# Weights by casting GpSimd DMAs beside Q, K and V, in place of plain loads in SP's queue cast by GpSimd

## The chip, the cores and the metric

The kernel runs on one core of one Trainium2 chip. The metric is the device time of one execution in microseconds (us); the median of three runs of the kernel before is 322.58 us (322.06 to 323.25). Engines are written as the profile writes them: PE (TensorE), with its weight loads PEld, DVE (VectorE), ACT (ScalarE), POOL (GpSimd) and SP (SyncE), which only issues DMAs here.

## The reference

Linear attention per head, a root-mean-square norm of each head's row, and then a two-layer network with an ELU between:

```python
kv  = einsum('bhsd,bhse->bhde', k, v)             # q, k, v: (8, 8, 576, 64) float32
out = einsum('bhsd,bhde->bhse', q, kv)
rms = sqrt(mean(out * out, axis=-1, keepdims=True) + 1e-06)
x   = (out / rms * g_norm)                        # heads side by side: (4608, 512)
h   = x @ w_in                                    # w_in: (512, 2048)
g   = where(h > 0, h, exp(minimum(h, 0)) - 1)
y   = g @ w_out                                   # w_out: (2048, 512), y: (4608, 512) float32
```

## The kernel before

**Tiling.** The 4608 tokens are worked on in nine groups of 512 tokens (G). Group b below 8 is the first 512 of the 576 positions of batch b; group 8 collects the last 64 positions of all eight batches. For each group the kernel computes attention (K'V of the batch, Q transposed by PE, Q times K'V, the norm, the result transposed to xT), then a first product with w_in (`mm1`, eight steps i of 256 of the 2048 columns, 16 matmuls each in bf16), the ELU, and a second product with w_out (`mm2`, 16 matmuls of 128x512 for each of four blocks of 128 tokens; `mm2_half(T, i)` does eight of them). The reduction index f of the second product, 0 to 15, runs over rows of w_out in blocks of 128; f below 4 lies in the first quarter of w_out, 12 to 15 in the last.

**Order.** A manual schedule is on: every engine runs its instructions in the order in which the program states them, and semaphores hold it only for data and for buffers. The attention of group T+1 is spread over the steps of the first product of group T by the dictionaries `steps`, and the second product of group T-1 over the same steps. For T = 0 the attention of group 1 stands in the first product of group 0 (q at step 2, kv at 3, se0 at 4, se1 at 6), and the second product of group 0 begins after step 7; after its first two halves PE transposes group 1's result (L284). Group 0's own attention (L396 to L492) is written out by hand, with `idle` matmuls on PE between its parts; its norm works on one joint tile `ss_all` for all four blocks.

**Loads.** All DMAs go out from SP, in float32, into a rotating set of six staging buffers `st` (L46, L72). The queue's order is: q, then halves of k and v of group 0 (L383 to L389), g_norm, w_in quarters 0 and 1 (`fetch_w_in`, L114), q, k and v of group 1 (`fetch`, L108), w_in 2 and 3, the four quarters of w_out (`fetch_w_out`, L122), group 2, group 3, and from then on a group for each group worked on, behind the stores of results. An issue waits until the staging buffer that it takes has been read.

**Casts.** Group 0 is cast to bf16 by DVE and ACT, part by part, as it lands. Everything else is cast by POOL through `copy_on` (L134), in the order w_in 0 and 1, group 1, w_in 2 and 3, w_out 0 to 3, group 2, and so on: four casts of 128x512 for q or a weight quarter (`cast_w_in`, L157; `cast_w_out`, L162), five for k or v.

**The ELU of a step** (L318 to L333): ACT takes exp of the step's PSUM tile (for odd steps of group 0 also relu), DVE takes min and subtract on `elu_e` (L325) and then a max or add into gT (L328), which is what the second product reads. The two PSUM tiles of `mm1` are given back by the last of these. One PSUM tile `at` (L170, two banks, a single buffer) serves all parts of the attention of groups 1 to 8 in turn.

Of the kernel before, what the change touches and what calls it, by code (L numbers as in the profile page):

```python
# [16 lines left out]
def kernel(  # L17
# [13 lines left out]
    nc = tc.nc  # L31
    P = 128
# [8 lines left out]
    KC = DM // P  # L41
# [1 line left out]
    NT = B + 1  # L43

    const = ctx.enter_context(tc.tile_pool(name="const", bufs=1))
    stage = ctx.enter_context(tc.tile_pool(name="stage", bufs=6))  # L46
    qkvp = ctx.enter_context(tc.tile_pool(name="qkvp", bufs=2))
    attp = ctx.enter_context(tc.tile_pool(name="attp", bufs=2))
    mlpg = ctx.enter_context(tc.tile_pool(name="mlpg", bufs=2))
# [18 lines left out]
    w_in_sb = const.tile([P, KC, DF], BF16, name="w_in_sb")  # L68
    w_out_sb = const.tile([P, FC, DM], BF16, name="w_out_sb")


    def stage_tile():  # L72
        return stage.tile([P, 2304], FP32, name="st", tag="st")

    raw, bf = {}, {}

    def fetch_q(b):

        st = stage_tile()[:, 0:2048]
        raw["q", b] = st  # L80
        if b < B:
            for s in range(2):
                nc.sync.dma_start(
                    out=st.rearrange("p (s h x) -> p s h x", s=2, h=4)[:, s],
                    in_=q[b].rearrange("(h s) r d -> s h r d", s=2)[s, :, 0:G, :].rearrange(
                        "h (p j) d -> p h (j d)", j=J
                    ),
                )
        else:
            sv = st.rearrange("p (i s h d) -> p i s h d", i=J, s=2, h=4)  # L90
            for t in range(B):
                for s in range(2):
                    nc.sync.dma_start(
                        out=sv[(t % 2) * 64 : (t % 2) * 64 + 64, t // 2, s],
                        in_=q[t].rearrange("(h s) r d -> s h r d", s=2)[
                            s, :, G:S, :
                        ].rearrange("h p d -> p h d"),
                    )

    def fetch_kv(name, src, b):  # L100

        st = stage_tile()
        raw[name, b] = st
        return st.rearrange("p (h x) -> p h x", h=4), src[b].rearrange(
            "h r d -> (h r d)"
        ).rearrange("(h p x) -> p h x", h=4, p=P)

    def fetch(b):  # L108
        fetch_q(b)
        for name, src in (("k", k), ("v", v)):  # L110
            out_, in_ = fetch_kv(name, src, b)
            nc.sync.dma_start(out=out_, in_=in_)

    def fetch_w_in(s):  # L114
        st = stage_tile()[:, 0:2048]
        nc.sync.dma_start(
            out=st.rearrange("p (c f) -> p c f", c=KC),
            in_=moe_w_in.rearrange("(c p) f -> p c f", p=P)[:, :, s * 512 : s * 512 + 512],
        )
        raw["wi", s] = st  # L120

    def fetch_w_out(s):  # L122
        st = stage_tile()[:, 0:2048]
        nc.sync.dma_start(
            out=st.rearrange("p (c f) -> p c f", c=KC),
            in_=moe_w_out.rearrange("(c p) f -> p c f", p=P)[:, 4 * s : 4 * s + 4, :],
        )
        raw["wo", s] = st

    def copy_on(eng, out_, in_):  # L130
        if eng is nc.scalar:
            nc.scalar.copy(out_, in_)
        else:
            eng.tensor_copy(out=out_, in_=in_)  # L134

    def q_tile(b):
        bf["q", b] = qkvp.tile([P, J, H, D], BF16, name="q_bf", tag="q")
        st = raw.pop(("q", b))
        if b < B:
            return st.rearrange("p (h j d) -> p j h d", h=H, j=J)  # L140
        return st.rearrange("p (j h d) -> p j h d", h=H, j=J)

    def kv_tile(name, b):
        bf[name, b] = qkvp.tile([P, RK, 4, D], BF16, name=f"{name}_bf", tag=name)
        return raw.pop((name, b)).rearrange("p (h j d) -> p j h d", h=4, j=RK)

    def cast_q(b, eng):
        sv = q_tile(b)
        for j in range(J):
            copy_on(eng, bf["q", b][:, j], sv[:, j])  # L150

    def cast_kv(name, b, eng):
        sv = kv_tile(name, b)
        for lo, hi in ((0, 2), (2, 4), (4, 6), (6, 8), (8, 9)):
            copy_on(eng, bf[name, b][:, lo:hi], sv[:, lo:hi])

    def cast_w_in(s, eng):  # L157
        st = raw.pop(("wi", s)).rearrange("p (c f) -> p c f", c=KC)
        for c in range(KC):
            copy_on(eng, w_in_sb[:, c, s * 512 : s * 512 + 512], st[:, c, :])  # L160

    def cast_w_out(s, eng):  # L162
        st = raw.pop(("wo", s)).rearrange("p (c f) -> p c f", c=KC)
        for c in range(KC):
            copy_on(eng, w_out_sb[:, 4 * s + c, :], st[:, c, :])


    xT = {}
# [5 lines left out]
    def kv_mm(T, kv_ps, u):  # L174

        for j in range(RK):
            for s in range(2):
                rows = slice(s * 64, s * 64 + 64)
                nc.tensor.matmul(  # L179
                    kv_ps[s][:, u * P : u * P + P],  # L180
                    lhsT=bf["k", T][rows, j, 2 * u : 2 * u + 2, :],
                    rhs=bf["v", T][rows, j, 2 * u : 2 * u + 2, :],
                    start=(j == 0),
                    stop=(j == RK - 1),
                )
# [192 lines left out]
    V, A, Q = nc.vector, nc.scalar, nc.gpsimd  # L378
# [6 lines left out]
    for u in range(2):  # L385
        for out_, in_ in halves:
            nc.sync.dma_start(
                out=out_[:, 2 * u : 2 * u + 2, :], in_=in_[:, 2 * u : 2 * u + 2, :]
            )  # L389
    g_src = bass.AP(tensor=g_norm.tensor, offset=g_norm.offset, ap=[[1, 64], [1, 1]])  # L390
    for i in range(2):
        nc.sync.dma_start(out=g_col[i * 64 : i * 64 + 64, :], in_=g_src)
    for s in range(2):
        fetch_w_in(s)

    q_st = q_tile(0)  # L396
    qt_ps = ps_m1.tile([P, 2, G], FP32, name="qt_ps", tag="mm1").rearrange(
# [4 lines left out]
    def idle(n):  # L402
        for _ in range(n):
            nc.tensor.matmul(idle_ps[:, 0, :], lhsT=ident, rhs=zeros, start=True, stop=True)  # L404
# [10 lines left out]
    kv_ps = [ps_m2.tile([P, DM], FP32, name="kv_ps", tag="mm2") for _ in range(2)]  # L415
    for u in range(2):
        for n, name in enumerate("kv"):
            for eng, js in ((V, slice(0, 5)), (A, slice(5, 9))):
                copy_on(
                    eng,  # L420
                    bf[name, 0][:, js, 2 * u : 2 * u + 2, :],
                    kv_st[n][:, js, 2 * u : 2 * u + 2, :],
                )
            if (u, n) == (0, 0):
                nc.vector.tensor_copy(out=qT0[:, 0:2, :], in_=qt_ps[:, 0:2, :])
                nc.scalar.copy(qT0[:, 2:4, :], qt_ps[:, 2:4, :])
        kv_mm(0, kv_ps, u)
        if u == 0:
            idle(6)
        for eng, l in ((V, 0), (A, 1)):  # L430
            ls = slice(l * 64, l * 64 + 64)
            for s in range(2):
                copy_on(
                    eng,
                    bd_kv[ls, 0, 2 * s + u, ls],
                    kv_ps[s][ls, u * P + l * 64 : u * P + l * 64 + 64],
                )
# [57 lines left out]
    def cast_all(b):  # L495
        cast_q(b, Q)
        if b < B:
            cast_kv("k", b, Q)
            cast_kv("v", b, Q)

    for s in range(2):
        cast_w_in(s, Q)
    fetch(1)
    cast_all(1)
    for s in range(2, 4):
        fetch_w_in(s)
    for s in range(2, 4):
        cast_w_in(s, Q)
    for s in range(4):
        fetch_w_out(s)  # L510
        cast_w_out(s, Q)
    fetch(2)
    at = attention(1)
    steps = {2: "q", 3: "kv", 4: "se0", 6: "se1"}
    for i in range(8):
        cols = (slice(0, 256), slice(256, 512)) if i == 0 else (slice(0, 512),)
# [69 lines left out]
```

## Time and profile before

| | |
|---|---|
| median of 3 runs | 322.58 us (322.06 to 323.25) |
| the profiled execution: its time, its span | 322.58 us, 320.4 us |
| busy: PE, DVE, ACT, POOL | 295.8, 179.2, 151.8, 78.4 us |
| DMA moved, and mean rate | 46.44 MB, 145 GB/s |
| first matmul of the first product | 22.03 us |
| first matmul of the second product | 45.48 us |
| DMA engines busy without a break | from 1 to about 62 us |
| granted TensorE clock | 1.000 |

The span runs from the first to the last instruction of the profiled execution; its own time is 2.18 us more. In the profile a line such as "L134 POOL CAST k_bf<-st" is a group of instructions: the line of the program (here that of the helper `copy_on`), the engine, the operation, what it writes and reads. A bracket such as "[2.28 <-POOL w_in_sb L134]" is the idle time of the engine just before it, and what is taken to have ended it; where an instruction waits for several things, the one that came last by the profile is named, which need not be the one that mattered. In the page's slices, each digit is the busy share of one fortieth of the span, about 8 us, in tenths.

### The profile page before, as it was taken

How to read it: one execution, taken by the hardware profiler on the slowest of the kernel's cores; microseconds unless marked ns; L12 is line 12 of the kernel's file. 1: busy time of each engine (PE TensorE's matmuls, PEld its weight loads, DVE VectorE, ACT ScalarE, POOL GpSimd, SP SyncE). 2: the span in 40 equal slices, each digit the busy share in tenths (PEclk: the TensorE clock that was granted, in tenths of full speed). 3: DMA queues.
4: the chain of work that ended last, by engine and by line, in shares of the span. 5: the costliest groups of instructions: out<-in, count | busy, mean ns of one | idle time of the engine just before them, and what ended most of it. 6: DMA issues, size and time to landing. Idle time of an engine off the chain costs nothing.

```text
span 320.4 us, 4746 instructions
## 1 busy us (share of the span) xinstructions
PE 295.8 (92%) x1905; PEld 149.7 (47%) x1941; DVE 179.2 (56%) x215; ACT 151.8 (47%) x215; POOL 78.4 (24%) x140
## 2 busy tenths in 40 slices
PE   8777686988899999999999999999999999999993
PEld 3443343554454445455545455545454545444441
DVE  3466584558447754775377537744874576454400
ACT  3654654356445544544544455444544545443220
POOL 0069998920026002600260045002000000000000
PEclk9999999999999999999999999999999999999999
DMA  7999999800193019302920392024201010101122
GB/s 255 354 376 389 386 374 376 314 0 2 61 354 119 25 68 349 139 4 89 368 102 2 108 363 88 0 90 99 78 1 65 2 65 2 65 0 65 68 65 65
DMA packets 28565, 46.44 MB, mean 145 GB/s; under 512 B 5504, under 2 KB 13696, under 8 KB 28544
## 3 DMA queue, kind: packets, MB, share of 16 engines
q1 hardware_dynamic: 28544, 46.14, 41.1%
q8 instruction: 15, 0.25, 0.3%
q14 instruction: 6, 0.05, 0.0%
HBM read 36.70 MB, written 9.44 MB: 144 GB/s over the span
## 4 chain that ended last, share of the span: by engine, by line
PE 78%; DMA 7%; DVE 5%; ACT 5%; issue 2%; SPq 1%; POOL 0%; DVEq 0%
PE o_ps L344 36%; PE h_ps L310 33%; DMA st<-in_moe_w_in_dram 5%; DMA st<-in_v_dram 3%; ACT elu_e L318 2%; PE at L179 2%; PE at L284 2%; DVE gT L328 2%; PE at L189 2%; PE at L201 2%; DVE ss L225 1%; DVE elu_e L325 1%; ACT sq L220 1%; DVE xs L235 1%; ACT elu_h L322 1%
## 5 line engine op out<-in xcount | busy, mean ns | idle before, releaser
L310 PE MATMUL h_ps<-xT,w_in_sb 128*128 128x512 bf16 (+1 forms) x564 | 133.8, 376 | 6.3 <-DVE gT L328 3.6
L344 PE MATMUL o_ps<-w_out_sb,gT 128*128 128x512 bf16 x562 | 133.9, 379 | 3.6 <-DVE gT L328 2.8
L318 ACT ACTIVATE elu_e<-h_ps 128x1024 bf16<-128x1024 f32 x72 | 73.5, 1020 | 50.2 <-PE h_ps L310 49.0
L344 PEld LDWEIGHTS <-gT 128*128 128x128 bf16 x576 | 56.2, 98 | 70.6 <-DVE gT L328 3.3
L328 DVE TENSOR_TENSOR gT<-elu_e,h_ps 128x1024 bf16<-128x1024 bf16 x68 | 83.0, 1221 | 7.1
L310 PEld LDWEIGHTS <-w_in_sb 128*128 128x128 bf16 x584 | 55.2, 98 | 65.2 <-issue 3.2
L325 DVE TENSOR_SCALAR elu_e<-elu_e 128x1024 bf16<-128x1024 bf16 x72 | 33.3, 462 | 87.8 <-ACT elu_e L318 87.8
L134 POOL CAST q_bf<-st 128x512 bf16<-128x512 f32 x32 | 18.9, 629 | 125.1 <-DMA st<-in_q_dram 103.4
L354 ACT COPY o_sb<-o_ps 128x512 f32<-128x512 f32 x36 | 21.0, 583 | 24.5 <-PE o_ps L344 24.5
L235 DVE TENSOR_TENSOR xs<-at,ss 128x1024 bf16<-128x1024 f32 x16 | 19.6, 1225 | 9.9 <-ACT ss L232 9.9
L220 ACT ACTIVATE sq<-at 128x1024 bf16<-128x1024 f32 (+1 forms) x18 | 17.5, 977 | 14.5 <-PE at L201 12.0
L225 DVE TENSOR_REDUCE ss<-sq 128x16 f32<-128x1024 bf16 x16 | 19.5, 1218 | 4.8 <-ACT sq L220 4.7
L134 POOL CAST k_bf<-st 128x512 bf16<-128x512 f32 (+1 forms) x35 | 20.1, 617 | 5.3 <-DMA st<-in_k_dram 4.5
L134 POOL CAST v_bf<-st 128x512 bf16<-128x512 f32 (+1 forms) x35 | 18.9, 584 | 0.7
L294 ACT ACTIVATE xT<-at,g_col 128x1024 bf16<-128x1024 bf16 x8 | 8.9, 1114 | 18.5 <-DVE xT L291 18.5
L231 ACT ACTIVATE ss<-ss,eps_col 128x16 f32<-128x16 f32 x16 | 4.9, 307 | 24.7 <-DVE ss L225 24.7
L404 PE MATMUL idle_ps<-zeros,ident 128*128 128x512 bf16 x43 | 13.3, 446 | 1.6 <-POOL ident masks.py:199 1.4
L264 ACT COPY qT<-at 128x1024 bf16<-128x1024 bf16 x8 | 8.1, 1012 | 12.3 <-DVE qT L263 12.3
L134 POOL CAST w_in_sb<-st 128x512 bf16<-128x512 f32 x16 | 9.8, 655 | 15.8 <-DMA st<-in_moe_w_in_dram 15.8
L179 PEld LDWEIGHTS <-k_bf 64*128 64x128 bf16 x288 | 8.2, 94 | 8.7 <-issue 4.1
L179 PE MATMUL at<-v_bf,k_bf 64*128 64x128 bf16 x252 | 8.3, 216 | 3.0 <-POOL w_in_sb L134 2.3
L201 PEld LDWEIGHTS <-qT 128*128 128x128 bf16 x128 | 8.4, 98 | 5.2 <-issue 1.9
(48 smaller groups left out, 117.6 us busy)
## 6 DMA issues: line engine op xcount, KB each, us to landing
st<-in_q_dram SPq DMA_DIRECT2D x16, 512.0 KB, 6.3
out_dram<-o_sb SPq DMA_DIRECT2D x16, 512.0 KB, 3.1
st<-in_k_dram SPq DMA_DIRECT2D x7, 1152.0 KB, 9.4
st<-in_v_dram SPq DMA_DIRECT2D x7, 1152.0 KB, 11.0
st<-in_moe_w_in_dram SPq DMA_DIRECT2D x4, 1024.0 KB, 12.8
st<-in_moe_w_out_dram SPq DMA_DIRECT2D x4, 1024.0 KB, 13.8
st<-in_k_dram SPq DMA_DIRECT2D x2, 576.0 KB, 7.2
st<-in_v_dram SPq DMA_DIRECT2D x2, 576.0 KB, 8.1
```

The costliest lines, as they stand in the source:

```text
L134: eng.tensor_copy(out=out_, in_=in_)
L179: nc.tensor.matmul(kv_ps[s][:, u * P : u * P + P], lhsT=bf["k", T][rows, j, 2 * u : 2 * u + 2, :], rhs=bf["v", T][rows, j, 2 * u : 2 * u + ...
L201: nc.tensor.matmul(ov[:, u, :, s, :], lhsT=qT[:, p, j * P : j * P + P], rhs=bd_kv[:, T, p, :], start=True, stop=True,)
L220: nc.scalar.activation(sq, se_ps, AF.Square)
L225: nc.vector.reduce_sum(out=ss, in_=sq.rearrange("p c (h e) -> p (c h) e", h=H), axis=AX.X)
L235: nc.vector.tensor_tensor(out=xs.rearrange("p c (h e) -> p (c h) e", h=H), in0=se_ps.rearrange("p c (h e) -> p (c h) e", h=H), in1=ss.to_b ...
L310: nc.tensor.matmul(h_ps[:, a, cs], lhsT=w_in_sb[:, c, f * P : f * P + P], rhs=x[:, c, cs], start=(c == 0), stop=(c == KC - 1),)
L318: nc.scalar.activation(e, h_ps, AF.Exp)
L325: nc.vector.tensor_scalar(out=e, in0=e, scalar1=1.0, scalar2=1.0, op0=ALU.min, op1=ALU.subtract)
L328: nc.vector.tensor_tensor(out=gT[T][:, 2 * i : 2 * i + 2, :], in0=e, in1=h, op=ALU.add if relu else ALU.max,)
L344: nc.tensor.matmul(o_ps[T, j], lhsT=gT[T][:, f, j * P : j * P + P], rhs=w_out_sb[:, f, :], start=(f == 0), stop=(f == FC - 1),)
L354: nc.scalar.copy(o_sb[T][:, j % 2, :], o_ps.pop((T, j)))
```

## The change

The weights no longer pass through staging and POOL's casts. Each quarter of w_in and w_out is loaded by one DMA issued from GpSimd's queue, which reads float32 and writes bf16 straight into `w_in_sb` or `w_out_sb`. The staging set shrinks from six buffers to three. In SP's queue, group 1 now follows group 0 directly. POOL's order becomes: a piece of group 0's V cast; w_in 0 and 1; q of group 1 cast; w_in 2 and 3; k and v of group 1 cast; w_out 0 to 3; then group 2's casts as before. The cast of the first half of group 0's V is split over three engines in place of two. The steps of group 1's attention and the norm chain are the same in both kernels.

```diff
-    stage = ctx.enter_context(tc.tile_pool(name="stage", bufs=6))
+    stage = ctx.enter_context(tc.tile_pool(name="stage", bufs=3))
...
-    def fetch_w_in(s):
-        st = stage_tile()[:, 0:2048]
-        nc.sync.dma_start(
-            out=st.rearrange("p (c f) -> p c f", c=KC),
-            in_=moe_w_in.rearrange("(c p) f -> p c f", p=P)[:, :, s * 512 : s * 512 + 512],
+    def load_w_in(s):
+        cols = slice(s * 512, s * 512 + 512)
+        nc.gpsimd.dma_start(
+            out=w_in_sb[:, :, cols], in_=moe_w_in.rearrange("(c p) f -> p c f", p=P)[:, :, cols]
         )
-        raw["wi", s] = st
...
+    def load_w_out(s):
+        fs = slice(4 * s, 4 * s + 4)
+        nc.gpsimd.dma_start(
+            out=w_out_sb[:, fs, :], in_=moe_w_out.rearrange("(c p) f -> p c f", p=P)[:, fs, :]
         )
...
-    for s in range(2):
-        fetch_w_in(s)
...
-            for eng, js in ((V, slice(0, 5)), (A, slice(5, 9))):
+            parts = ((V, slice(0, 5)), (A, slice(5, 9)))
+            if (u, n) == (0, 1):
+                parts = ((V, slice(0, 4)), (A, slice(4, 7)), (Q, slice(7, 9)))
+            for eng, js in parts:
...
+    fetch(1)
     for s in range(2):
-        cast_w_in(s, Q)
-    fetch(1)
-    cast_all(1)
+        load_w_in(s)
+    cast_q(1, Q)
     for s in range(2, 4):
-        fetch_w_in(s)
-    for s in range(2, 4):
-        cast_w_in(s, Q)
+        load_w_in(s)
+    cast_kv("k", 1, Q)
+    cast_kv("v", 1, Q)
     for s in range(4):
-        fetch_w_out(s)
-        cast_w_out(s, Q)
+        load_w_out(s)
     fetch(2)
```

More of the change, by code (lines that the diff above doesn't have):

```diff
@@ L112, in fetch @@
             nc.sync.dma_start(out=out_, in_=in_)
-    def fetch_w_in(s):
-        st = stage_tile()[:, 0:2048]
-        nc.sync.dma_start(
-            out=st.rearrange("p (c f) -> p c f", c=KC),
-            in_=moe_w_in.rearrange("(c p) f -> p c f", p=P)[:, :, s * 512 : s * 512 + 512],
-        )
-        raw["wi", s] = st
[L122 to L126, printed above, removed]
+    def load_w_in(s):
+        cols = slice(s * 512, s * 512 + 512)
+        nc.gpsimd.dma_start(
+            out=w_in_sb[:, :, cols], in_=moe_w_in.rearrange("(c p) f -> p c f", p=P)[:, :, cols]
+        )
+    def load_w_out(s):
+        fs = slice(4 * s, 4 * s + 4)
+        nc.gpsimd.dma_start(
+            out=w_out_sb[:, fs, :], in_=moe_w_out.rearrange("(c p) f -> p c f", p=P)[:, fs, :]
         )
-        raw["wo", s] = st
     def copy_on(eng, out_, in_):
@@ L155, in cast_kv @@
             copy_on(eng, bf[name, b][:, lo:hi], sv[:, lo:hi])
[L157 to L165, printed above, removed]
     xT = {}
```

## The prediction

> **What bounds the kernel now.** I read four views in this order. First the page's slices and the table of windows, to see in which stage TensorE is not full:
>
> ```profile
> 20.00:36.00 16.00, 11.41 (x107) 6.88 (x108) 8.09 (x12) 8.94 (x13) 13.58 (x24) 1.00 1.06 387
> 36.00:52.00 16.00, 10.90 (x62) 5.09 (x60) 11.49 (x13) 8.64 (x13) 14.29 (x23) 1.00 1.06 381
> 86.00:118.00 32.00, 31.74 (x211) 16.36 (x215) 19.12 (x22) 15.84 (x22) 7.78 (x14) 1.00 0.40 140
> ```
>
> Columns are the stretch, its length, busy time of PE, PE's weight loads, DVE, ACT and POOL, then clock, DMA share and GB/s. From 86 us on PE is busy 31.7 of 32 us with DMA at 40%: the change, which touches only loads and their casts, can win or lose nothing there. From 20 to 52 us PE has 9.7 us of idle, the DMA engines are saturated (share above 1, 381 to 387 GB/s) and POOL casts without a break. The change acts here, and before.
>
> Second, the chain that ended last, for what starts this stage:
>
> ```profile
> 3.34 9.12 DMA st<-in_v_dram
> 12.49 0.57 DVE v_bf L134
> ...
> 20.01 14.44 DMA st<-in_moe_w_in_dram
> 34.50 0.62 POOL w_in_sb L134
> 35.20 1.69 PE h_ps L310 x7
> ```
>
> The second half of group 0's V lands at 12.46 us, and from it a gapless chain runs to the first product at 22.03. The second piece looks as if w_in held everything until 34.5. The wait itself says less, so third, PE in that stretch:
>
> ```profile
> 33.86 1.18 PE L179 MATMUL at<-v_bf,k_bf 64*128 64x128 bf16 x36 [2.28 <-POOL w_in_sb L134]
> 35.20 1.67 PE L310 MATMUL h_ps<-xT,w_in_sb 128*128 128x512 bf16 x7 [0.16 <-POOL w_in_sb L134]
> 40.22 1.89 PE L310 MATMUL h_ps<-xT,w_in_sb 128*128 128x512 bf16 x8 [1.17 <-DVE gT L328]
> 45.48 3.19 PE L344 MATMUL o_ps<-w_out_sb,gT 128*128 128x512 bf16 x14
> 51.51 0.60 PE L344 MATMUL o_ps<-w_out_sb,gT 128*128 128x512 bf16 x2 [2.84 <-DVE gT L328]
> ```
>
> The product at 33.86 reads no w_in. It needs the one `at` buffer back from ScalarE's qT copy (32.70 + 1.01 = 33.71) and v_bf (cast by 32.12): the 2.28 us are ScalarE's, behind DVE. Only 0.16 us is a wait for w_in. The other gaps end with DVE's gT. So **the first product is paced by ScalarE and VectorE, not by weights**; weights merely arrive in time. How much in time, POOL says:
>
> ```profile
> 42.59 5.37 POOL L134 CAST w_out_sb<-st 128x512 bf16<-128x512 f32 x8 [0.42 <-DMA st<-in_moe_w_out_dram]
> ```
>
> w_out is complete at 47.96. PE starts the second product at 45.48; at 0.216 us each (8 take 1.73), its matmul f=12, first to need the last quarter, is due at 48.1. **Slack of the last weight: 0.1 us** until f=12, and 3.5 us until 51.5, when gT of the last step comes.
>
> **The Trainium skill.** "DMA: Bandwidth & Descriptors", section "SWDGE vs HWDGE vs iDMA": a casting DMA must come from GpSimd, whose descriptors are software-made, in a queue of its own; section "Issuing engines are not separate DMA queues": it shares the same 16 DMA engines. This trace has one data queue, so sharing is not shown; that the 16 are full until 62 us is. Section "Queues, rings and completion order": each engine takes turns between queues packet by packet. Packets here are rows: 8,192 of 1 KB for q, 8,192 of 2.25 KB for k and v, 4,096 of 2 KB for the weights fit the page's counts. "SBUF — State Buffer", section "Who interferes with whom": a VectorE operation in a two-port mode and a GpSimd operation exclude each other. The trace agrees: elu_e's 128x1024 TENSOR_SCALAR takes 0.42 us with POOL idle (65 to 84 us) but 0.66, 0.58, 0.69, 0.72, 0.88, 0.42, 0.59, 0.42 in the first product.
>
> **The change, part by part.**
>
> Removed: 32 weight casts on POOL of about 0.61 us, 19.6 us, all beside other work. They hold PE for 0.16 us and lengthen elu_e by 1.6 us in sum (the eight above less 8 x 0.42), of which steps 0, 2, 4 and 6 lie on the chain: 0.24 + 0.27 + 0.46 + 0.17 = 1.1 us. But POOL still casts group 1 and, earlier than before, group 2 in this stage, so about half stays: **gain 0.5 us** (0 to 1.6).
>
> Added: eight DMA issues on POOL. The trace has none; the skill's DMA page, "Specifications", gives about 1 us to the first byte. I take 1 us of POOL each. Floor 0; ceiling 2 us each, should VectorE's two-port operations hold them up. Behind them on POOL stand cast_q(1), then k's and v's casts, for which PE's q and kv steps wait.
>
> Group 0's V cast split in three: POOL gets 128x256 (0.40 us by the page's form of that size), ScalarE's part shrinks from four rows to three (0.15 us). This is V's first half; the second half's landing sets the chain, so 0.
>
> Moved, at the start: w_in 0 and 1 stood behind V's second half in SP's queue. Now POOL issues them after its piece of the V cast: V's first half lands at 9.4, cast to 9.9, first byte at 10.9. By then 3.06 of the 3.41 MB of group 0 are in (windows: 2.03 by 8 us, then 354 GB/s). The last 0.35 MB shares: 2.25 KB packets against 2 KB, 0.53 of 0.36 MB/us, 1.85 us, to 12.75 in place of 11.9. **Loss 0.85 us** on the chain, nothing beside it to hide it. Bounds: 0 if the weights' first byte is late, 3.1 if their queue gets three quarters.
>
> Moved, in the order of loads: stage falls from six buffers to three, so q of group 2 is issued after cast_q(1), k and v after their casts; SP's stores (first at 58.84) stand behind them and have time. w_out waits on POOL behind v's cast of group 1, and then shares with group 2's loads, which formerly stood behind it. By turns, at 0.386 MB/us, weights get 2/3 beside q and 0.47 beside k and v, and landing comes 1 us after the last byte (0.6 for V, 2.4 for w_in 3 in this trace):
> - w_in 0 and 1 (2.10 MB) have 0.31 by 12.75, the rest takes 7.0 us beside q: 19.7. q is in at 20.1, landed 21.1, cast (2.3 us) 23.4.
> - w_in 2 and 3 issue then, bytes from 24.4. k alone to 23.2; v alone to 24.4, then shared to 27.9; POOL casts them by 28.5 and 31.8. Before: 32.12. The kv step at 33.9 is not held.
> - w_in 2 is in at 29.5, w_in 3 at 33.6, beside q of group 2. Needed at 35 and 40: no stall.
> - w_out follows at 33.6: 0.62 MB beside the rest of q to 36.0, then 2.08 beside k and v (2.36 MB) to 47.5, then the last 1.49 beside q of group 3 (released by cast_q(2) near 39.4) in 5.8 us: 53.3, **landed 54.3**.
>
> w_out 0 and 1 land near 39 and 45, on time. w_out 2 lands near 50, w_out 3 at 54.3, so PE's f=12 is held to 54.4, and its four matmuls end at 55.26. Before, the two for gT began at 51.51 and the transposes that follow at 51.95. **Loss 3.3 us**, in which the 0.85 and the 0.5 above vanish: they shift PE to that same wait. What is late next is nothing: after it PE has the same dense order.
>
> Sum: span 320.4 + 3.3 = 323.7. The profiled execution took 322.58, 2.18 more than its span, and is also the median. 323.7 + 2.2 = **325.9 us**.
>
> **The rivals.**
> - *The weights' queue gets most of each engine* (several rows a packet). At three quarters, V is done 3.1 us later; w_out lands near 53, and PE, 3.1 less 0.7 late, is there at about the same time. 322.6 + 2.4 = 325.0. Against it: nothing in the trace tells.
> - *It gets little, or the cast slows the engines.* At one third w_in 3 lands at 43 (3 us late) and w_out 3 near 61: 322.6 + 10 = 332.5. For it: rows of 2 KB turn into 1 KB; against: the bytes read[...] are the same.
> - *Everything arrives in time, and the relief counts: faster.* The casting transfers write half the bytes; if two queues together move more than now, w_out 3 lands by 50.5 and V is not late. Then 1.6 us of elu_e contention, less what stays: 322.6 - 1.6 = 321.0 at best. It decides from a combined rate of 420 GB/s: 19.4 MB moved by 53.3, in place of by 50. The trace's best window is 391.
> - *It doesn't do what its words say:* attention of group 1 inside the first product and the joint norm chain already stand in the kernel before, so they give 0; the loads are changed for sure. No case of its own.
>
> **Numbers.** Chances: forecast 0.45, large share 0.20, small share 0.15, in time 0.20. A measurement tells about 0.5% (1.6 us) from no change. Slower by more: most of the forecast and of the large share, all of the small, 0.70. Within: 0.20. Faster: half of the in-time case, 0.10. Range 321.5 to 332.5: it leaves out the best of the in-time case and the slow half of the small share.
>
> **What would show it.** Right: PE waits some 5 us at L344 for the w_out DMA near 49 to 54; V of group 0 is cast about 13.3, the first product starts near 22.9; POOL busy falls by 20 us less the issues; PE after 60 us as before. Wrong: w_out landed before 50.5 (the order of loads then costs nothing), the first product starting at 22.0, or a wait for w_in at steps 4 or 6.

## The result, and the profile after

The changed kernel takes 333.45 us (median of 4 runs, 332.56 to 334.02), the kernel before 322.52 us beside it: a ratio of 1.033 (95% interval 1.030 to 1.037). The profiled execution took 334.02 us with a span of 331.9 us, 11.5 us more than before, at a mean granted clock of 0.969 in place of 1.000. The forecast of 325.9 us had the direction; its range ended 1 us too early.

First the stages. This is the table of windows of the kernel after; the columns are as in the prediction (stretch, length, busy PE, PEld, DVE, ACT, POOL, then clock, DMA share, GB/s):

```profile
20.00:36.00 16.00, 11.65 (x107) 7.22 (x109) 8.19 (x13) 8.95 (x13) 8.60 (x14) 0.96 1.08 289
36.00:52.00 16.00, 11.04 (x54) 4.99 (x55) 10.15 (x13) 9.12 (x14) 9.12 (x17) 0.93 1.13 290
52.00:68.00 16.00, 9.56 (x40) 4.65 (x40) 1.27 (x2) 1.70 (x2) 7.57 (x14) 0.58 0.70 204
```

And the row of the third stretch in the kernel before:

```profile
52.00:68.00 16.00, 15.06 (x126) 8.39 (x128) 6.94 (x8) 7.02 (x10) 12.99 (x24) 1.00 0.69 250
```

Between 20 and 52 us PE is busy for about as long as before, though at a lower clock and, in the second row, with 54 instructions in place of 62. The loss lies in the third row: PE is idle for 6.4 of 16 us and runs at a clock of 0.58; before, it was idle for 0.9 us at full clock. The GB/s are not comparable with those of before: a casting load is counted with what it writes, half of what it reads (42.24 MB moved in place of 46.44, with 36.70 MB read from HBM in both).

The chain that ended last, in order of time (start, duration, what), kernel after:

```profile
7.42 10.08 DMA st<-in_q_dram
17.62 2.31 POOL q_bf L130 x4
20.47 11.49 DMA st<-in_v_dram
32.01 2.64 POOL v_bf L130 x5
...
36.79 23.47 DMA w_out_sb<-in_moe_w_out_dram
60.30 1.87 PE o_ps L330 x4
```

Before, the chain ran through V of group 0 and w_in into the first product. Now it runs through q of group 1, its cast, v of group 1, its cast, and the last quarter of w_out. L330 is the line that was L344. PE's timeline shows how the second product takes the four quarters (a step of the first product shows as eight matmuls of 128x512, not the 16 of the description above; a few records are missing, so a count can be short):

```profile
47.06 1.03 PE L330 MATMUL o_ps<-w_out_sb,gT 128*128 128x512 bf16 x3
50.61 1.02 PE L330 MATMUL o_ps<-w_out_sb,gT 128*128 128x512 bf16 x4 [2.52 <-DMA w_out_sb<-in_moe_w_out_dram]
54.82 1.87 PE L330 MATMUL o_ps<-w_out_sb,gT 128*128 128x512 bf16 x4 [3.18 <-DMA w_out_sb<-in_moe_w_out_dram]
60.30 1.87 PE L330 MATMUL o_ps<-w_out_sb,gT 128*128 128x512 bf16 x4 [3.61 <-DMA w_out_sb<-in_moe_w_out_dram]
61.96 1.91 PE L270 MATMUL at<-ident,xs 128*128 128x128 bf16 x16
63.67 2.83 PE L330 MATMUL o_ps<-w_out_sb,gT 128*128 128x512 bf16 x8
66.33 1.89 PE L296 MATMUL h_ps<-xT,w_in_sb 128*128 128x512 bf16 x8
```

The two lines of the kernel before to set beside the last ones:

```profile
51.95 1.06 PE L284 MATMUL at<-ident,xs 128*128 128x128 bf16 x16
54.57 1.89 PE L310 MATMUL h_ps<-xT,w_in_sb 128*128 128x512 bf16 x8
```

Two things are to be seen. Each quarter of w_out but the first is waited for, and f=12 stands at 60.30, where the prediction had 54.4. In the kernel before f=12 ran without a wait and only f=14 waited, until 51.51; since two matmuls take 0.43 us, that is as if f=12 had stood at 51.1. And the same four matmuls that take 1.02 us at 50.61 take 1.87 us at 54.82 and 60.30, the sixteen transposes 1.91 us in place of 1.06: the half clock. From f=12 to the next group's first step it is 6.03 us; in the kernel before, reckoned so, it was 54.57 - 51.1 = 3.5 us. So 9.2 us of lateness and 2.5 us of slow clock make 11.7 us, against a span longer by 11.5.

What put w_out so late is on the queues. POOL, kernel after:

```profile
9.38 0.65 POOL L130 CAST v_bf<-st 128x256 bf16<-128x256 f32 x1 [8.07 <-DMA st<-in_v_dram]
9.98 2.00 POOL L116 DMA_DIRECT2D w_in_sb<-in_moe_w_in_dram  x2
...
32.01 2.64 POOL L130 CAST v_bf<-st 128x512 bf16<-128x512 f32 x5 [2.39 <-DMA st<-in_v_dram]
34.59 2.97 POOL L122 DMA_DIRECT2D w_out_sb<-in_moe_w_out_dram  x4
```

And the issues of SP, kernel after:

```profile
19.94 0.37 SPq L112 DMA_DIRECT2D st<-in_k_dram  x1
20.47 0.39 SPq L112 DMA_DIRECT2D st<-in_v_dram  x1
...
29.65 0.37 SPq L112 DMA_DIRECT2D st<-in_k_dram  x1
34.68 0.37 SPq L112 DMA_DIRECT2D st<-in_v_dram  x1
```

What this waited for, from the view of waits of SP:

```profile
SPq L112 <- DMA st<-in_q_dram: 9.6, 1, 9.6
SPq L112 <- POOL q_bf L130: 2.3, 1, 2.3
```

K and V of group 1 leave at 19.94 and 20.47, not at 12.8, when the buffers of k and v of group 0 had been read. K waits until q of its own group has landed (17.5) and POOL has cast it (19.91): so it takes the staging buffer that this q held (with six buffers, in the fourth experiment, the wait is gone). V lands at 32.0, POOL casts it and only then issues w_out, at 34.59. By that time k and v of group 2 are in the other queue. The bytes of w_out come later still. The view of DMA queues by stretches counts packets: q0 is GpSimd's queue, q1 SP's. From 34.6 to 38.7 us:

```profile
q1 hardware_dynamic: 1024, 1.61, 107.3%
```

And from 38.7 to 60 us (packets, MB, the time that the packets took):

```profile
q0 software_dynamic: 2112, 2.10, 57.9%
q1 hardware_dynamic: 2326, 3.87, 55.5%
```

GpSimd's queue moves nothing for 4.2 us after its first w_out issue at 34.59, while SP's fills the engines. For w_in it was the same: issued at 9.98, first packet at 14.7. Then the two share the time of the engines by halves. By the times of the packets w_out's bytes run from 38.8 to 59.9 us: 4.19 MB read in 21.1 us, or 0.199 MB/us, beside SP's 3.87 MB, so 0.52 of the bytes. The quarters land at 46.0, 50.6, 54.8 and 60.3.

### The profile page after: what moved, and what is told of

It reads as the page before. It is cut to its first block, busy times and chain, and to the rows that moved or that the text cites. A ratio compares the mean times of both kernels' runs of the same rounds, so it can differ in the third digit from the quotient of the medians.

```text
span 331.9 us, 4712 instructions
## 1 busy us (share of the span) xinstructions
PE 301.3 (91%) x1905; PEld 152.2 (46%) x1941; DVE 177.2 (53%) x215; ACT 151.9 (46%) x215; POOL 65.2 (20%) x117
## 2 busy tenths in 40 slices
DMA packets 28565, 42.24 MB, mean 127 GB/s; under 512 B 5504, under 2 KB 17792, under 8 KB 28544
## 3 DMA queue, kind: packets, MB, share of 16 engines
q0 software_dynamic: 4224, 4.19, 7.5%
HBM read 36.70 MB, written 9.44 MB: 139 GB/s over the span
## 4 chain that ended last, share of the span: by engine, by line
PE 75%; DMA 15%; DVE 3%; ACT 2%; POOL 2%; issue 1%; SPq 0%; DVEq 0%; POOLq 0%
PE o_ps L330 36%; PE h_ps L296 32%; DMA w_out_sb<-in_moe_w_out_dram 7%; DMA st<-in_q_dram 5%; DMA st<-in_v_dram 3%; PE at L270 2%; PE at L165 2%; PE at L175 2%; PE at L187 1%; DVE gT L314 1%; ACT elu_e L304 1%; POOL v_bf L130 1%; POOL q_bf L130 1%; DVE elu_e L311 0%; POOL w_out_sb L122 0%
## 5 line engine op out<-in xcount | busy, mean ns | idle before, releaser
L330 PE MATMUL o_ps<-w_out_sb,gT 128*128 128x512 bf16 x561 | 136.9, 384 | 10.2 <-DMA w_out_sb<-in_moe_w_out_dram 9.3
L330 PEld LDWEIGHTS <-gT 128*128 128x128 bf16 x576 | 56.9, 99 | 79.0 <-issue 13.0
L311 DVE TENSOR_SCALAR elu_e<-elu_e 128x1024 bf16<-128x1024 bf16 x72 | 32.0, 445 | 90.6 <-ACT elu_e L304 90.6
L221 DVE TENSOR_TENSOR xs<-at,ss 128x1024 bf16<-128x1024 f32 x16 | 19.6, 1225 | 9.9 <-ACT ss L218 9.9
L206 ACT ACTIVATE sq<-at 128x1024 bf16<-128x1024 f32 (+1 forms) x18 | 17.5, 977 | 14.1 <-PE at L187 11.6
L165 PEld LDWEIGHTS <-k_bf 64*128 64x128 bf16 x288 | 9.0, 99 | 8.8 <-issue 4.6
L277 DVE TENSOR_SCALAR xT<-at,g_col 128x1024 bf16<-128x1024 bf16 x8 | 6.0, 746 | 11.4 <-PE at L270 11.4
## 6 DMA issues: line engine op xcount, KB each, us to landing
st<-in_v_dram SPq DMA_DIRECT2D x7, 1152.0 KB, 11.5
```

The source lines that it names most:

```text
L165: nc.tensor.matmul(kv_ps[s][:, u * P : u * P + P], lhsT=bf["k", T][rows, j, 2 * u : 2 * u + 2, :], rhs=bf["v", T][rows, j, 2 * u : 2 * u + ...
L206: nc.scalar.activation(sq, se_ps, AF.Square)
L221: nc.vector.tensor_tensor(out=xs.rearrange("p c (h e) -> p (c h) e", h=H), in0=se_ps.rearrange("p c (h e) -> p (c h) e", h=H), in1=ss.to_b ...
L311: nc.vector.tensor_scalar(out=e, in0=e, scalar1=1.0, scalar2=1.0, op0=ALU.min, op1=ALU.subtract)
L330: nc.tensor.matmul(o_ps[T, j], lhsT=gT[T][:, f, j * P : j * P + P], rhs=w_out_sb[:, f, :], start=(f == 0), stop=(f == FC - 1),)
```

## The experiments

All times are medians, beside runs of the kernel before on the same chip; the changed kernel itself has the ratio 1.033. The experiments ran on three other chips, where the kernel before had medians of 323.28 to 323.73 us, so across kernels it is the ratios that compare. None of the kernels leaves out a part of the computation.

**1. Issue w_out before the casts of k and v.** If POOL's order alone makes w_out late, this brings it forward; if the sharing does, little is won.

```diff
-    cast_kv("k", 1, Q)
-    cast_kv("v", 1, Q)
     for s in range(4):
         load_w_out(s)
+    cast_kv("k", 1, Q)
+    cast_kv("v", 1, Q)
```

> The changed kernel with one move: the four w_out issues stand on POOL before the casts of k and v of group 1. Theory A (w_out is late because its queue stood empty from 34 to 38 us, behind v's cast and some 4 us to the first byte, and then shares the engines with groups 2 and 3): its bytes follow w_in 3 without a gap at 34, so the last quarter lands near 55 to 56 in place of 60.3, PE waits some 4 to 5 us less, part of the half clock goes, 327 to 328.5 us. Theory B (a casting transfer simply takes more of the engines than its bytes say): the queue was never really empty, the last quarter still lands near 60, 333 us.

Measured: 328.28 us, ratio 1.014 (1.010 to 1.018). w_out is issued at 20.54, 14 us earlier, but its last quarter lands only 5 us earlier. PE's timeline:

```profile
50.26 2.75 PE L330 MATMUL o_ps<-w_out_sb,gT 128*128 128x512 bf16 x11
55.36 0.59 PE L330 MATMUL o_ps<-w_out_sb,gT 128*128 128x512 bf16 x2 [2.35 <-DMA w_out_sb<-in_moe_w_out_dram]
```

And its waits:

```profile
PE at L165 <- POOL v_bf L130: 4.5, 4, 3.2
```

Now w_out shares with k and v of group 1, so these are late (v is cast at 33.57 to 36.9), PE waits 4.5 us for them in the kv step, and the second product begins at 50.26 in place of 47.06. Moving the issues forward takes away a good half of the loss. What is left goes with loads that are late in another place: v of group 1, and still the last quarter of w_out.

**2. Let w_out have the engines alone.** SP is held by a small DMA that reads the last quarter of w_out, so that group 2 leaves after it.

```diff
         load_w_out(s)
+    hold = const.tile([P, 16], BF16, name="hold")
+    nc.sync.dma_start(out=hold, in_=w_out_sb[:, FC - 1, 0:16])
     fetch(2)
```

> The changed kernel with SP held after group 1: a DMA of 4 KB that reads the last quarter of w_out stands ahead of group 2 in SP's queue, so group 2 is issued only when w_out is in. Theory A: w_out has the engines to itself from 38.4, 4.19 MB at 0.386 MB/us take 10.9 us, it lands near 50, before PE needs its second half; PE then waits for gT again, 323 to 325 us. Theory B: it takes clearly longer than 11 us even alone, lands at 53 or later, 326 us or more. If group 2, now 9 us of loads after 50, comes too late for the steps of the next first product, PE waits there instead, near 60 to 66.

Measured: 324.53 us, ratio 1.002 (1.000 to 1.005). The hold goes out at 49.25, when the last quarter is in. W_out is issued at 34.88, as late as in the changed kernel, its packets run from 36.3 to 48.9, and it has landed at 49.2. PE's timeline:

```profile
47.24 3.19 PE L330 MATMUL o_ps<-w_out_sb,gT 128*128 128x512 bf16 x13
52.74 0.90 PE L330 MATMUL o_ps<-w_out_sb,gT 128*128 128x512 bf16 x2 [2.31 <-DVE gT L314]
53.44 1.91 PE L270 MATMUL at<-ident,xs 128*128 128x128 bf16 x16
```

There is no wait for w_out any more; the one that ends last is gT, as before the change. **Taking the sharing with group 2 away takes the whole loss away**: the ratio goes from 1.033 to 1.002. So POOL's order and the late issue cost nothing that shows here as long as w_out has the engines to itself, and the parts of the loss that these experiments remove overlap: they can't be added up. The transposes at 1.91 us show that the half clock was there too, after a wait of only 2.31 us. A casting load isn't slow: 4.19 MB took 12.6 us here, 0.33 MB/us read, and in the ninth experiment four quarters in a row took 10.2 us (29.7 to 39.9), 0.41 MB/us.

**3. Keep PE busy in its waits.** Matmuls of zeros (9, 13 and 19, about as long as the waits) stand between the quarters; they move no data and change no wait.

```diff
-    mm2_half(0, 0)
-    mm2_half(0, 1)
+    for f, n in ((0, 9), (4, 13), (8, 19), (12, 0)):
+        mm2(0, 0, f, f + 4)
+        for _ in range(n):
+            nc.tensor.matmul(warm_ps[:, 0, :], lhsT=ident, rhs=zeros, start=True, stop=True)
```

> The changed kernel with matmuls on zeros (9, 13 and 19 of 0.216 us) in PE's three waits for w_out, into a PSUM tile of its own. Nothing about the loads changes. Theory A has two terms: 9.2 us of lateness and some 2.5 us because PE runs the work after it at half clock from 60 to 66 us: the second goes, 330.5 to 331.5 us, the last quarter still lands near 60.3. Rival: the half clock is only a label of idle time, PE would have waited anyhow: 333 us, or a little more if the matmuls overrun the landings.

Measured: 331.26 us, ratio 1.022 (1.019 to 1.025), below the interval of the changed kernel. PE's timeline:

```profile
59.45 1.02 PE L330 MATMUL o_ps<-w_out_sb,gT 128*128 128x512 bf16 x4 [0.57 <-DMA w_out_sb<-in_moe_w_out_dram]
60.31 1.06 PE L270 MATMUL at<-ident,xs 128*128 128x128 bf16 x16
```

PE still waits for every landing, but the same work then takes 1.02 and 1.06 us, and the next step begins 3.48 us after f=12 in place of 6.03. So the half clock is worth 2.5 us, and it comes from PE's waits. (In this profile the span is 3.4 us shorter; the other 0.85 is f=12 at 59.45, since w_out was issued 0.7 us earlier, which the zeros do not touch.)

**4. Six staging buffers, as before the change.** This takes away the wait of k for the buffer of q.

```diff
-    stage = ctx.enter_context(tc.tile_pool(name="stage", bufs=3))
+    stage = ctx.enter_context(tc.tile_pool(name="stage", bufs=6))
```

> The changed kernel with six staging buffers again. k of group 1 was issued at 19.9 us only, when POOL had cast q of group 1, whose buffer it took: with six it goes out near 8. Theory A: v of group 1 lands near 29 in place of 32, w_out is issued near 32 in place of 34.6, but shares with as much of the other queue as before: the last quarter lands near 58, 330.5 to 332 us. Rival (three buffers held the other queue back and so helped w_out): more of groups 2 and 3 is queued ahead of time, the last quarter lands after 60, 333.5 us or more.

Measured: 331.35 us, ratio 1.022 (1.020 to 1.025). k leaves at 7.90. POOL's timeline has w_out's issue:

```profile
31.47 2.96 POOL L122 DMA_DIRECT2D w_out_sb<-in_moe_w_out_dram  x4
```

And PE's timeline of the same kernel its last wait:

```profile
57.33 1.86 PE L330 MATMUL o_ps<-w_out_sb,gT 128*128 128x512 bf16 x4 [2.69 <-DMA w_out_sb<-in_moe_w_out_dram]
```

w_out leaves 3.1 us earlier and lands 3.0 us earlier. The buffers are 3 us of the loss; a new wait of 1.8 us for w_in at step 2 lies ahead of w_out's and costs nothing here.

**5 and 6. One half of the change alone.** The fifth kernel keeps w_in by casting loads and puts w_out back into SP's queue with POOL's casts (six buffers); the sixth is the kernel before with only w_out by casting loads, at the place of its casts.

```diff
     for s in range(4):
-        load_w_out(s)
+        fetch_w_out(s)
+        cast_w_out(s, Q)
     fetch(2)
```

> One part alone: w_in by casting GpSimd DMAs as in the changed kernel, w_out through SP, staging (six buffers) and POOL's casts as before, between group 1 and group 2. Theory A: the casting loads of w_in cost nothing by themselves; they share with group 1 until about 36 us, w_out has landed near 44.5 and is cast near 47, about when PE needs it: 322 to 324 us, the kernel before within 0.5%. Theory B (casting loads are slow by themselves): w_in or group 1 comes late, PE waits in the first product, 326 us or more.

```diff
     for s in range(4):
-        fetch_w_out(s)
-        cast_w_out(s, Q)
+        load_w_out(s)
     fetch(2)
```

> The other part alone: w_in through SP and POOL's casts as before, only w_out by casting GpSimd DMAs, issued where its casts stood, after the casts of w_in 2 and 3 (37.4 us). Theory A: first bytes near 41, then half of the engines beside groups 2 and 3: the last quarter lands near 61 to 63, as late as in the changed kernel or later: 333 to 337 us. If the loss came from the loads of w_in or from group 1's place in the queue instead, 323 us.

Measured: 335.84 us, ratio 1.039 (1.035 to 1.042), for w_out alone, as expected: it leaves at 37.77, and PE waits for it four times, 10.6 us in sum. Its last wait, on PE's timeline of the sixth kernel:

```profile
62.58 1.87 PE L350 MATMUL o_ps<-w_out_sb,gT 128*128 128x512 bf16 x4 [2.00 <-DMA w_out_sb<-in_moe_w_out_dram]
```

w_in alone gave 325.82 us, ratio 1.008 (1.005 to 1.011), 1.8 us above the expected range. Nothing waits for w_out, but PE's timeline of the fifth kernel shows a cost that had not been counted:

```profile
22.75 3.65 PE L309 MATMUL h_ps<-xT,w_in_sb 128*128 128x256 bf16 x24 [0.48 <-DMA w_in_sb<-in_moe_w_in_dram]
28.52 1.90 PE L309 MATMUL h_ps<-xT,w_in_sb 128*128 128x512 bf16 x7 [2.13 <-DMA w_in_sb<-in_moe_w_in_dram]
```

With six buffers k and v of group 1 leave early, at 8.08 and 9.58, and share with w_in 0 and 1. So w_in has the same weakness. In the changed kernel the small number of buffers protects it: the fourth experiment differs in that number alone, and there the wait for w_in appears. **The w_out half alone makes the whole loss.**

**7. A load by itself.** Two extra loads of a w_in quarter from GpSimd's queue at moments when POOL has nothing else and the DMA engines little: one casting, one plain float32.

```diff
+        if T in (3, 4):
+            lone = const.tile([P, KC, 512], BF16 if T == 3 else FP32, name=f"lone{T}")
+            nc.gpsimd.dma_start(
+                out=lone, in_=moe_w_in.rearrange("(c p) f -> p c f", p=P)[:, :, 0:512]
+            )
```

> The disputed cost by itself: the changed kernel, with two more loads of a w_in quarter from GpSimd's queue at moments when the DMA engines are idle (in the third and fourth of the later groups, after POOL's casts): one casting, one float32 to float32. Nothing reads them. Theory A: both move 1.05 MB at about the same pace, 2.7 us of engine time, and land 4.5 to 5.5 us after the issue, of which about 2 are before the first byte. Theory B: the casting one lands at least 1.5 us after the other. Time 333 to 334 us, as the changed kernel.

The DMA view of the seventh kernel (KB written each, us from issue to landing):

```profile
lone<-in_moe_w_in_dram POOLq DMA_DIRECT2D x1, 1024.0 KB, 8.0
lone<-in_moe_w_in_dram POOLq DMA_DIRECT2D x1, 512.0 KB, 7.5
```

The two are alike, as expected, but both take 2 to 3.5 us more than expected. The engines were not quite idle: SP issued a store of a result at 115.27 and at 146.79, beside both. By the packets, the casting load runs from 117.6 to 122.3 us after an issue at 115.10, the plain one from 149.3 to 154.0 after 146.42: 4.7 us each for 1 MB read, with the store's last packets in the first microsecond, and 2.5 and 2.9 us before the first packet. (The kernel as a whole took 334.40 us, ratio 1.034, 1.028 to 1.040, like the changed one.)

**8. Without POOL's piece of the V cast.** Then POOL issues w_in at once, and it shares with all of k and v of group 0: the loss that the prediction counted as 0.85 us, made larger.

```diff
-            if (u, n) == (0, 1):
-                parts = ((V, slice(0, 4)), (A, slice(4, 7)), (Q, slice(7, 9)))
```

> The changed kernel without POOL's piece of group 0's V cast. That piece made POOL wait for V before it issued w_in 0 and 1; now they are issued at about 1.3 us and their bytes come from 4 to 5 us, beside k and v of group 0. By turns, V lands near 17 in place of 12.5 and the first product starts near 26 to 27. Theory A: that is absorbed, because PE then reaches the second product about 4 us later and still has to wait for w_out, which lands near 60 to 62: 333 to 335.5 us. If a late start counts beside the late w_out (they add): 337 us or more. If the weights' queue gets nothing beside the other, the start stays at 22 to 23.

Measured: 337.07 us (2 runs), ratio 1.041 (1.035 to 1.047). V lands at 17.47 in place of 12.46, and the first product starts still later than was expected, by PE's timeline:

```profile
28.54 3.64 PE L296 MATMUL h_ps<-xT,w_in_sb 128*128 128x256 bf16 x24
```

5.0 us of the 5.7 are V's; the rest goes with a clock of one half until 22 us, where the changed kernel had it from 11 to 14. V of group 1 is later too, so w_out leaves at 37.52 and f=12 stands at 63.55, 3.2 us later. The profiled span grows by 2.5 us (334.4 against 331.9) and not by 5.7: the two delays do not add, the later wait swallows most of the first. The median is above the 335.5 that was expected for this case, because w_out itself landed at 63.5, where 60 to 62 was expected. The piece of a cast is a gate, and without it the loss that was feared is real.

**9, 10 and 11. Is anything left to win?** The ninth has six buffers, w_out early and the hold; the tenth is the second with 25 matmuls of zeros in PE's waits; the eleventh puts the same 25 into the kernel before, as a control. The edit of the zeros, alike in both:

```diff
-        mm1(0, i, cols, relu=(i % 2 == 1))()
+        rest = mm1(0, i, cols, relu=(i % 2 == 1))
+        warm({1: 4, 3: 8, 6: 4}.get(i, 0))
+        rest()
...
-    mm2_half(0, 1)
+    mm2(0, 0, 8, 14)
+    warm(9)
+    mm2(0, 0, 14, FC)
```

> The changed kernel with six staging buffers, w_out issued ahead of the casts of k and v of group 1, and SP held on the last quarter of w_out before group 2. Theory A: the weights' queue never runs empty and shares only with group 1 until 28 us; w_out lands near 44 to 45, v of group 1 near 28.5, group 2 near 54: no wait for a load on PE after 22 us. POOL casts nothing between 32 and 46, so elu_e is at its 0.42 us there: 320.5 to 322.5 us, the kernel before or up to 0.5% faster. If POOL's relief is worth nothing or the half clock in PE's gaps comes back: 322.5 to 324.

> The kernel with group 2 held behind w_out, and besides 25 matmuls on zeros in PE's gaps of the first product and ahead of the last two of the first half of the second (4, 8, 4 and 9), so that PE doesn't fall to half clock after a gap. Theory: with w_out in time and the clock kept, what remains of the change is POOL's relief and the start at 21.8: 320 to 321.8 us, faster than the kernel before by 0.3 to 0.8%. If the relief is worth nothing: as the kernel before with the same matmuls.

> The control: the kernel before with the same 25 matmuls at the same places. If half clock after gaps costs it now and then (its runs on one chip went from 322.6 to 325 with granted clocks from 0.998 to 0.989), the median falls to 322 to 323 us and the spread closes; it can't fall below its best runs, 322 us. If the matmuls get in the way, 323.5 to 325.

Measured: the ninth 324.68 us, ratio 1.004 (1.000 to 1.007), a miss. w_out lands at 45.2 and is never waited for, but w_in is, 1.17 us ahead of the first product and 1.92 us at step 2. The tenth 323.31 us, ratio 1.001 (0.999 to 1.003), also a miss. PE's timeline of the tenth:

```profile
48.90 0.59 PE L330 MATMUL o_ps<-w_out_sb,gT 128*128 128x512 bf16 x2 [0.92 <-DMA w_out_sb<-in_moe_w_out_dram]
49.33 2.10 PE L507 MATMUL warm_ps<-zeros,ident 128*128 128x512 bf16 x9
51.27 0.59 PE L330 MATMUL o_ps<-w_out_sb,gT 128*128 128x512 bf16 x2
51.70 1.06 PE L270 MATMUL at<-ident,xs 128*128 128x128 bf16 x16
```

The transposes begin at 51.70; in the profile of before it was 51.95. The eleventh, on the same chip, took 322.47 us, ratio 0.997 (0.995 to 0.999), its transposes begin at 51.58:

```profile
51.14 0.60 PE L344 MATMUL o_ps<-w_out_sb,gT 128*128 128x512 bf16 x2 [1.01 <-DVE gT L328]
51.58 1.06 PE L284 MATMUL at<-ident,xs 128*128 128x128 bf16 x16
```

It is the only kernel here that beats the kernel before, by 0.3%, and it holds nothing of the change. No kernel with the change was faster than the kernel before, and the intervals of the tenth and the eleventh touch. That does not show that the lighter POOL is worth nothing, as DVE's timelines tell. The last gT of the tenth, and then of the eleventh:

```profile
49.98 0.69 DVE L314 TENSOR_TENSOR gT<-elu_e,elu_h 128x1024 bf16<-128x1024 bf16 x1 [0.52 <-ACT elu_h L308]
```

```profile
50.03 1.05 DVE L328 TENSOR_TENSOR gT<-elu_e,elu_h 128x1024 bf16<-128x1024 bf16 x1 [0.52 <-ACT elu_h L322]
```

In the tenth gT is ready at 50.67, 28.5 us after its first product began (22.17); in the eleventh at 51.08, 29.3 us after (21.74). But in the tenth w_out came late once more, the nine zeros stood behind it, and PE was busy with them until 51.27. So up to 0.6 us of the relief lay unused there. What it would be worth without that wait, no run here shows.

## Why the prediction was wrong: its steps

**The mechanism was right.** w_out stands behind v's cast on POOL, then shares with group 2, and PE waits for it in group 0's second product. The first experiment shows POOL's order, the second the sharing, the sixth that this half is the whole loss. The share was near too: w_out's bytes came at 0.199 MB/us, where the prediction's turns by packets make 4.19 MB in 19.7 us, 0.213.

**What failed is the size of the w_out term: "landed 54.3" was 60.3, and "the same dense order" after it ran in part at half clock.** Together they make 8.2 us of span (331.9 against 323.7), in four terms of the sum.

- *"k alone to 23.2".* This supposes that k of group 1 can leave once the buffers of k and v of group 0 are free, about 12.8. In the program its issue waits for q of group 1 and that q's cast, until 19.94. v's cast ended at 34.6 in place of 31.8: 2.8 us. The fourth experiment, with six buffers, gives 3.0.
- *"about 1 us to the first byte"* (the Trainium skill, "DMA: Bandwidth & Descriptors", "Specifications"). Measured 4.2 us for w_out in the changed kernel, 1.4 us in the second experiment, 2.5 and 2.9 us in the seventh. The measurement decides. Here 4.2 in place of 1 is 3.2 us; 0.8 of it had been covered in the prediction, where w_out's bytes followed w_in 3 without a gap.
- *"landed 54.3".* Transfer of w_out 21.1 us in place of 19.7: 1.4 us more; landing 0.4 us after the last packet in place of 1: 0.6 less. 2.8 + 3.2 - 0.8 + 1.4 - 0.6 = 6.0 us: 60.3.
- *"after it PE has the same dense order".* The order is the same, the clock is not. After waits of 3.18 and 3.61 us PE worked at half clock until about 65 us: 2.5 us, which the third experiment took away. The Trainium skill, "TensorE: Matmul & The Clock Gate", "What's actually happening", says that the clock falls back after some 3.4 us of idle and returns after as long a busy stretch. The traces do not follow this for single waits. Half clock was granted after waits of 1.63 us (sixth experiment, from about 12 us), 1.74 us (changed kernel, 11 to 14 us), 2.31 us (second) and 3.18 us. It was not after waits of 2.84 us (profile of before) and 2.98 us (ninth). So the length of one wait doesn't settle it.

6.0 + 2.5 is 8.5, less 0.3 that PE makes good later.

**The loss of 0.85 us at the start did not happen.** V's second half is cast at 12.49 in both kernels, since the weights' first bytes came only after 14 us. The bound "0 if the weights' first byte is late" was the case. Yet the first product did start at 22.85, where 22.9 was forecast. That is a hit by accident: it goes with the half clock between 11 and 14 us. The sixth experiment, whose start is that of the kernel before, had this too:

```profile
22.90 3.64 PE L316 MATMUL h_ps<-xT,w_in_sb 128*128 128x256 bf16 x24
```

In the first three experiments, with the clock at 1, the first product starts at 21.75 to 21.77. That is no gain of POOL's piece of V's cast: in the eleventh, which has no such piece, it starts at 21.74.

**The relief of POOL came, and was swallowed.** POOL's busy time fell by 13.2 us: some 19.6 us of weight casts went, and 6.45 us for eight issues (0.8 us each; 1 was forecast) and 0.65 us for the piece of V came. elu_e's excess in the first product fell from 1.6 to 0.5 us. In the changed kernel the last gT was ready at 52.5, and w_out's last quarter at 60.3, so nothing of this could show. The tenth against the eleventh shows no gain in time either, but there the zeros were in the way; the forecast of 0.5 us is neither confirmed nor refuted.

**The rivals.** "It gets little" named 332.5 us, close to the measured time, by another road: it needed w_in 3 at 43 us, from a share of one third or casting that slows the engines. w_in 3 landed at 34.9 (34.6 was forecast), the share was a half, and in the seventh experiment the casting load took as long as the plain one. "Most of each engine" and "in time" are out by the share and by PE's waits. (The 3.1 us of that first rival is 2.9 by its own numbers: 0.35 MB at a quarter of 0.36 MB/us takes 3.9 us in place of 1.0. Nothing hangs on it.)

What stays open: why the first packet came 1.4 us after the issue in the second and tenth experiments, when nothing else was moving, and more than 4 us after it beside SP's loads; what decides when the clock falls after a wait of 2 to 3 us; and how w_out would do by plain loads from GpSimd's queue. No run here separates these.

## What to carry to other kernels

A load that is moved to a queue of its own loses its place in the order: it shares the engines with whatever the other queue has out, even with data that nobody needs for another 10 us, so either hold the later loads back or keep one queue. Before you credit a freed engine, look at what ends last in that stage; here it was the load of w_out, and in the kernel before DVE's gT. And where TensorE waits, look at the granted clock behind the wait too: here it added 2.5 us to waits of 3.18 and 3.61 us.

## What the runs showed of the hardware

- From the issue of a load by GpSimd to its first packet it took 1.4 us with nothing else moving (second and tenth experiments), 2.5 and 2.9 us beside a store (seventh), and 4.2 to 4.7 us beside SP's loads (changed kernel). An issue kept POOL busy for 0.74 to 1.0 us.
- A casting load (1 MB float32 read, 0.5 MB bf16 written) took 4.7 us from its first to its last packet, a plain one, which writes twice as much, 4.7 us too: the time goes by what is read. Both stood beside the end of a store.
- Beside SP's loads, GpSimd's queue got 0.52 of the bytes read (4.19 of 8.06 MB in 21 us).
- Filling waits on PE with 25 matmuls of zeros made the kernel before 0.3% faster (0.995 to 0.999).
